# One decoding step with its gradients: ScalarE issues the stores that Pool issued, TensorE's instructions stand in written order, and a group's output sums follow a head's o sums

## The chip, the cores and the metric

The kernel runs on one core of a Trainium2 chip. A core has five engines, each with an instruction stream of its own: TensorE (PE; its weight loads appear as PEld) multiplies matrices into the PSUM accumulators, VectorE (DVE) and ScalarE (ACT) work elementwise and reduce, GpSimd (Pool) and SyncE (SP) do little but issue transfers here. Sixteen DMA engines move data between the device memory and the on-chip memory SBUF. An instruction on one engine that needs another's result waits for a semaphore, and whatever stands behind it on its own engine waits with it.

The metric is the time of one execution on the device in microseconds: 738.34 us in the median of three runs, 738.0 to 738.96.

## The reference

One token attends over a cache of 8192 positions with 32 heads, beside a gated MLP, and all gradients are wanted. With D = 640, Dh = 128, F = 1728, all bf16:

```python
xn = layernorm(x)
q  = (xn @ wq) per head                      # wq [640, 32*128]
p  = softmax(q . k_cache[h] * Dh**-0.5)      # k_cache, v_cache [32, 8192, 128]
o  = p @ v_cache[h]
out = x + concat(o) @ wo + (silu(xn @ w1) * (xn @ w3)) @ w2
# outputs: out, and the gradients of x, k_cache, v_cache, wq, wo, w1, w3, w2 for a given grad_out
```

For one head the gradients of the caches are outer products: dV[j] = p[j] * do, where do is the head's share of grad_out through wo, and dK[j] = u[j] * q, with u[j] = p[j] * (dp[j] - sum(p * dp)) and dp = V . do. K, V, dK and dV have 2 MB each per head, so per head 4 MB are read and 4 MB written. All weights are read once and a gradient of their size is written.

## The kernel before

**Layout.** A head's K lies in SBUF as 128 partitions x 64 positions x 128 elements, each partition one contiguous run of 16384 B in memory; V, dK and dV are alike. K has three buffers (`kp`) and V two (`vp`); dK and dV share four (`op`, tag "o", tile `ot`), in which W2's parts stand at the start.

**A head.** `product` (L333) forms scores: VectorE multiplies half of K (or V) by the broadcast q (or do) into `T` (L347), and TensorE adds up the 64 columns of that half with eight matmuls by the identity (L349), into `psS` or `psDP`. `row_max` and `exps` make the exponentials; ScalarE computes `E` (L392) and TensorE the total (L393). `probs` makes the probabilities `P2`, and on ScalarE `Pf` (L401). `attend` (L404) sums o with 64 matmuls over V's blocks, `row_dots` the sum p * dp (L418 on TensorE), `dscores` the vector `U2`, its copy `Uf` and 64 matmuls for dq over K's blocks (L429). `outer` (L352) writes dV or dK in two halves: of each half's 32 positions ScalarE makes eight with eight small activations (L362), VectorE the rest in one instruction (L369). `turn_wq` transposes the head's columns of Wq (L435), `weights` forms the head's rows for the weight gradients (L444 to L459), `keep_dq` stores the dq row (L465).

**The loop** (L631) runs two heads at a time, shifted: while head h is finished as `c`, the scores of head h + 1, `n`, are formed. In its order stand S of n, first half; P of c; dV first half; the sum p * dp and o; the Wq transposes; S second half; dV second half; `dscores`; dK first half; DP of n; dK second half; `exps(n)`; DP second half; `weights(c)`.

**Groups.** Four heads form a group. Wo is loaded per group (`load_wo`, two buffers), Wq for eight heads (`load_wq`, two buffers). Preparing the next group (`prep_steps`: q sums over Wq, L257, transposes of Wo, L247, do sums, L269) and finishing the last one are cut into steps, and `gap()` (L608) runs one step of the oldest at five marked places of a head. `finish_steps` (L296) starts in the first head of the next group: `on_sums` copies the group's o into `on` and `on_bf` and adds its 20 matmuls to the output (L292), then ScalarE overwrites Wo by its gradient, four activations (L301) and a store, and Wq by its gradient, five activations (L308), with a store after every second group. Three such stores of the last groups are put off (`late`) to head 29.

**Order.** `manual_schedule` (L98) keeps the written order on VectorE, SP, Pool and ScalarE. TensorE's order is made by the framework's scheduler, except at a few matmuls marked `keep_in_program_order`. Buffers are handed on by semaphores.

**Transfers.** SP issues all loads: x, W1, W2, W3, then Wq, Wo, K, V as buffers come free; a load waits on SP for its buffer, and later loads wait behind it. Pool issues all stores, each as soon as its tile is made, but for heads 30 and 31 (`TAIL`), whose dK and dV SP stores in halves (L374), the last group's Wo gradient (L706) and dx (L729). ScalarE issues only two small transfers, grad_out (L103) and out (L734). K 2 can be loaded only when W3's gradient has left its buffer (`load_k(2)` after the dW3 store, L600), V 1 after the dW1 store (L589).

Of the kernel before, what the change touches and what calls it, by code (L numbers as in the profile page):

```python
# [21 lines left out]
def kernel(  # L22
# [34 lines left out]
    NG = H // GH  # L57
    ORDERED = {mybir.EngineType.DVE, mybir.EngineType.SP, mybir.EngineType.Pool, mybir.EngineType.Activation}
    GW = 8
# [38 lines left out]
    with tc.manual_schedule(engines=ORDERED):  # L98
# [23 lines left out]
        def store(dst, src, later=False):  # L122
            if later:
                late.append((dst, src))
            else:
                nc.gpsimd.dma_start(dst, src)

# [154 lines left out]

        def on_sums(g):
            G_ = grp[g]
            wo_g = G_["wo"]
            on = small.tile([P, GH], F32, name="on")
            nc.scalar.copy(on[:], G_["on_ps"])
            on_bf = small.tile([P, GH], BF16, name="on_bf")
            nc.scalar.copy(on_bf[:], on[:])
            for r in range(GH):  # L290
                for ci in range(NC):
                    nc.tensor.matmul(accbank[:, OUT0 + ci:OUT0 + ci + 1], lhsT=wo_g[:, r, ci * P:(ci + 1) * P],  # L292
                                     rhs=on_bf[:, r:r + 1], start=False, stop=True, skip_group_check=True)
            return on

        def finish_steps(g):  # L296
            G_ = grp[g]
            wo_g = G_["wo"]
            on = on_sums(g)
            for r in range(GH):  # L300
                nc.scalar.activation(wo_g[:, r, :], g_bc_bf[:], ACTF.Copy, scale=on[:, r:r + 1])  # L301
                if r == 1:
                    yield
            store(dwo_v[g], wo_g[:], g == NG - 2)
            yield
            b, k = divmod(g, HB)
            for ci in range(NC):
                nc.scalar.activation(G_["wq"][:, ci, :], G_["dqbc"][:].rearrange("p h d -> p (h d)"),  # L308
                                     ACTF.Copy, scale=xn_col[:, ci:ci + 1])
                if ci == 2:  # L310
                    yield
            if g < NG - HB and k == HB - 1:
                store(dwq_v[:, :, b * GW * DH:(b + 1) * GW * DH], G_["wq_all"][:], g == NG - HB - 1)
# [52 lines left out]
        def outer_v(st, vec, w2, dst, h, half, j1):  # L366
# [6 lines left out]
            if h >= H - TAIL:  # L373
                nc.sync.dma_start(dst[h][:, j0:j0 + JH, :], rows[:, j0:j0 + JH, :])  # L374
            elif half:
                nc.gpsimd.dma_start(dst[h], rows)  # L376

# [92 lines left out]
        def mlp_steps():  # L470
# [13 lines left out]
            def gate_sums(wi, wt):  # L484
                for b, rows in blocks:
                    for ci in range(NC):
                        mm = nc.tensor.matmul(gu_ps[0:rows, wi, b:b + 1], lhsT=wt[:, ci, b * P:b * P + rows],
                                              rhs=xn_col_bf[:, ci:ci + 1], start=(ci == 0), stop=(ci == NC - 1))
                        if wi:
                            tc.keep_in_program_order(mm)  # L490

# [56 lines left out]

            def w2_grad(k):
                b0, nb, nfull, w2c = w2_parts[k]  # L550
                for b, rows in blocks[b0:b0 + nb]:
                    for ci in range(NC):
                        nc.tensor.matmul(accbank[:, OUT0 + ci:OUT0 + ci + 1], lhsT=w2c[0:rows, b - b0, ci * P:(ci + 1) * P],
                                         rhs=hcol_bf[0:rows, b:b + 1], start=False, stop=True, skip_group_check=True)
                    nc.scalar.activation(w2c[0:rows, b - b0, :], g_bc_bf[0:rows, :], ACTF.Copy, scale=hcol[0:rows, b:b + 1])
                    if b in (1, 3, 5, 7, 9):
                        yield
                nc.gpsimd.dma_start(dw2_v[:, b0:b0 + nfull, :], w2c[:, 0:nfull, :])
                if nfull < nb:
                    nc.gpsimd.dma_start(out_8[NF * P:F, :], w2c[0:REST, nfull, :])  # L560

# [37 lines left out]
            grad_v(1, w3t, 4, 1)  # L599
            nc.gpsimd.dma_start(dw3_v, w3t[:])  # L600
            load_k(2)
# [29 lines left out]
        for h in range(H - 1):  # L631
# [32 lines left out]
            if n:  # L664
                exps(n)
                product(n, "DP", 1)
            weights(c)
# [28 lines left out]
        keep_dq(c)  # L696
        on = on_sums(g)
        outer(c, c.q, c.U2, None, dkc, H - 1, 1)
# [66 lines left out]
```

## Time and profile before

| | before |
|---|---|
| median of three runs | 738.34 us (738.0 to 738.96) |
| profiled execution, span | 739.3 us, 0.13% above the median; the profile gives no other time of it |
| moved | 303.69 MB (151.34 MB read and as many written), 411 GB/s in the mean |
| DVE | 627.9 us busy, 85% |
| PE | 550.8 us, 75% |
| ACT | 469.0 us, 63% |
| POOL | 45.7 us, 6% |
| dK and dV stores issued by Pool | 60, 533 ns each, 19.4 us from issue to landing (median) |
| loads of K, of V on SP | 32 each, 25.4 and 21.4 us to landing |

A profile shows one execution. Its slices cut the span in 40 equal parts; a digit is the busy share of a slice in tenths. A group of instructions is named by its line, engine and tiles, output before input. A row of waits names the waiting group, an arrow and what it waited for, then the us in total, how often and the longest. The chain follows the work that ended last back through what released each step. A landing is the time from the issue of a transfer until its completion reached the semaphore.

The page's list of DMA queues has one by hardware (q1), fed by SP, one by software (q0), fed by Pool, and a second one by hardware (q10) with the two small transfers of ScalarE. The trace also has every DMA packet with queue, size and duration, and every completion count of a transfer; a transfer that uses all 16 DMA engines has 16 such counts, the last of them is its landing.

### The profile page before, as it was taken

What the parts mean: (1) busy time and instruction counts of PE and PEld (TensorE: products, weight loads), DVE (VectorE), ACT (ScalarE), POOL (GpSimd) and SP (SyncE); (2) the same over time, 40 slices, a digit from 0 to 9 for tenths busy, and PEclk for the clock granted to TensorE, in tenths of its full rate; (3) what the DMA queues carried; (4) which work ended last, traced back from release to release, by engine and by line L of the source; (5) the groups of instructions that cost most, each with busy time, mean ns of one, the idle gap of its engine ahead of it and who ended that gap; (6) DMA issues with size and microseconds to landing.
All of it is one profiled execution on the core that took longest, in us unless ns stands there. A gap on an engine that the chain in (4) does not pass through costs nothing.

```text
span 739.3 us, 15756 instructions
## 1 busy us (share of the span) xinstructions
PE 550.8 (75%) x6497; PEld 323.2 (44%) x6513; DVE 627.9 (85%) x708; ACT 469.0 (63%) x1395; POOL 45.7 (6%) x87
## 2 busy tenths in 40 slices
PE   4777787777778888685488976788188888789671
PEld 3454444434435454343255444445055444445340
DVE  3689999989699997998389996999469998899992
ACT  2394567686567774694366964686167866668552
POOL 0010000000000100000000100000000000000100
PEclk9697888777976787658696698867687678866875
DMA  9999999999999999999999999999989999999995
GB/s 325 418 396 318 402 430 429 430 425 430 428 432 427 426 430 429 427 431 424 396 402 424 426 431 426 426 433 422 429 341 418 427 425 434 426 430 425 418 413 204
DMA packets 28390, 303.69 MB, mean 411 GB/s; under 512 B 2861, under 2 KB 4591, under 8 KB 10911
## 3 DMA queue, kind: packets, MB, share of 16 engines
q1 hardware_dynamic: 16514, 160.39, 52.3%
q0 software_dynamic: 11792, 142.30, 45.7%
q8 instruction: 51, 0.84, 0.4%
q14 instruction: 21, 0.16, 0.1%
q10 hardware_dynamic: 12, 0.00, 0.0%
HBM read 151.34 MB, written 151.34 MB: 409 GB/s over the span
## 4 chain that ended last, share of the span: by engine, by line
DMA 59%; DVE 23%; PE 13%; SPq 2%; issue 1%; ACT 1%; DVEq 0%; ACTq 0%
DMA Kt<-in_A_k_cache_dram 30%; DMA out_dram<-wo_g 12%; DVE T L347 11%; DMA wq_g<-in_A_wq_dram 8%; DVE ot L369 8%; PE psS L349 5%; DMA out_dram<-ot 5%; DMA wo_g<-in_A_wo_dram 4%; PE ob L407 2%; PE ob L429 1%; DVE DP_sb L414 1%; DVE S_sb L380 1%; PE dx_ps L569 1%; SPq L152 1%; PE ps_t L247 1%
## 5 line engine op out<-in xcount | busy, mean ns | idle before, releaser
L349 PE MATMUL psDP<-T,ident_bf 128*128 128x512 bf16 x512 | 184.6, 523 | 64.8 <-DVE T L347 64.8
L349 PEld LDWEIGHTS <-ident_bf 128*128 128x128 bf16 x1024 | 121.0, 121 | 233.3 <-issue 178.8
L362 ACT ACTIVATE ot<-qs_g,Uf 128x128 bf16<-128x128 bf16 x496 | 151.5, 389 | 34.4 <-DVE Uf L427 26.4
L347 DVE TENSOR_TENSOR T<-Kt,qs_g 128x4096 bf16<-128x4096 bf16 x64 | 146.4, 2289 | 21.7 <-DMA Kt<-in_A_k_cache_dram 20.5
L349 PE MATMUL psS<-T,ident_bf 128*128 128x512 bf16 x512 | 146.5, 438 | 19.0 <-DVE T L347 18.9
L362 ACT ACTIVATE ot<-do_g,Pf 128x128 bf16<-128x128 bf16 x504 | 153.9, 389 | 1.0
L347 DVE TENSOR_TENSOR T<-Vt,do_g 128x4096 bf16<-128x4096 bf16 x64 | 145.9, 2280 | 8.8 <-DMA Vt<-in_A_v_cache_dram 8.8
L369 DVE TENSOR_TENSOR ot<-qs_g,U 128x3072 bf16<-128x3072 bf16 (+1 forms) x64 | 113.1, 1768 | 6.1 <-DMA out_dram<-ot 6.1
L369 DVE TENSOR_TENSOR ot<-do_g,P 128x3072 bf16<-128x3072 bf16 (+1 forms) x64 | 112.8, 1762 | 1.1
L376 POOL DMA_DIRECT2D out_dram<-ot x60 | 32.0, 533 | 584.3 <-DVE Uf L427 247.3
L429 PEld LDWEIGHTS <-Kt 128*128 128x128 bf16 x2048 | 58.8, 100 | 12.6 <-issue 10.9
L429 PE MATMUL ob<-U,Kt 128*128 128x1 bf16 x2048 | 58.0, 164 | 1.6 <-DVE U L422 1.5
L407 PEld LDWEIGHTS <-Vt 128*128 128x128 bf16 x2048 | 57.3, 98 | 0.0
L407 PE MATMUL ob<-P,Vt 128*128 128x1 bf16 x2048 | 57.2, 163 | 0.0
L401 ACT ACTIVATE Pf<-E,rZ 128x16 f32<-128x16 f32 x32 | 9.8, 307 | 57.4 <-DVE rZ L397 57.3
L448 ACT ACTIVATE dq_diag<-ident_bf,odq 128x128 bf16<-128x128 bf16 x32 | 12.8, 399 | 47.7 <-DVE odq L444 47.7
L392 ACT ACTIVATE E<-S_sb,negM 128x64 f32<-128x64 f32 x32 | 11.0, 345 | 41.5 <-DVE negM L389 41.5
L422 DVE SCALAR_TENSOR_TENSOR U<-DP_sb,sm,P 128x128 bf16<-128x128 f32 x32 | 11.1, 348 | 27.3 <-PE sm L418 27.3
L257 PE MATMUL ps_q<-wq_g,xn_col_bf 128*128 128x512 bf16 x32 | 11.3, 469 | 30.4 <-DMA wq_g<-in_A_wq_dram 29.4
L384 PE MATMUL sm<-ident_f,mrow 128*128 128x128 f32 x64 | 19.6, 399 | 16.9 <-DVE mrow L382 16.4
L252 ACT COPY woT<-ps_t 128x512 bf16<-128x512 bf16 x40 | 22.9, 573 | 14.2 <-PE ps_t L247 14.2
L393 PEld LDWEIGHTS sm<-rsum,ones_fc 128*128 128x128 f32 x64 | 18.2, 298 | 19.4 <-ACT E L392 12.0
(151 smaller groups left out, 508.3 us busy)
## 6 DMA issues: line engine op xcount, KB each, us to landing
out_dram<-ot POOLq DMA_DIRECT2D x60, 2048.0 KB, 19.4
Kt<-in_A_k_cache_dram SPq DMA_DIRECT2D x32, 2048.0 KB, 25.4
Vt<-in_A_v_cache_dram SPq DMA_DIRECT2D x32, 2048.0 KB, 21.4
out_dram<-ot SPq DMA_DIRECT2D x8, 1024.0 KB, 12.1
wq_g<-in_A_wq_dram SPq DMA_DIRECT2D x4, 1280.0 KB, 35.1
wo_g<-in_A_wo_dram SPq DMA_DIRECT2D x8, 640.0 KB, 10.9
out_dram<-wo_g POOLq DMA_DIRECT2D x7, 640.0 KB, 21.3
out_dram<-wq_g POOLq DMA_DIRECT2D x3, 1280.0 KB, 30.9
```

The costliest lines, as they stand in the source:

```text
L252: nc.scalar.copy(woT[:], ps_t[:])
L257: nc.tensor.matmul(ps_q[:], lhsT=xn_col_bf[:, ci:ci + 1].to_broadcast([P, P]), rhs=wq_g[:, ci, :], start=(ci == 0), stop=(ci == NC - 1))
L347: nc.vector.tensor_tensor(T[:], src[:, :, ds_], vec[:, ds_].unsqueeze(1).to_broadcast([P, J, DHH]), ALU.mult)
L349: nc.tensor.matmul(ps[:], lhsT=ident_bf[:], rhs=T[:, :, RUN * i:RUN * (i + 1)], start=(half == 0 and i == 0), stop=(half == 1 and i == DHH ...
L362: nc.scalar.activation(st.ot[:, j1 - ACT_J + j].rearrange("p a b -> p (a b)"), vec, ACTF.Copy, scale=wf[:, half, j:j + 1])
L369: nc.vector.tensor_tensor(st.ot[:, j0:j1], vec.rearrange("p (a b) -> p a b", b=2).unsqueeze(1).to_broadcast([P, n, DH // 2, 2]), w2[:, j0: ...
L376: nc.gpsimd.dma_start(dst[h], rows)
L384: nc.tensor.matmul(st.sm[:, 8:8 + P], lhsT=mrow[:].to_broadcast([P, P]), rhs=ident_f[:], start=True, stop=True, skip_group_check=True)
L393: nc.tensor.matmul(st.sm[:, 3:4], lhsT=ones_f, rhs=rsum[:], start=True, stop=True, skip_group_check=True)
L407: mm = nc.tensor.matmul(st.ob[:, 0:1], lhsT=st.V[:, j, :], rhs=st.P2[:, j, 0:1], start=(j == 0), stop=(j == J - 1), skip_group_check=True)
L429: nc.tensor.matmul(st.ob[:, 1:2], lhsT=st.K[:, j, :], rhs=st.U2[:, j, 0:1], start=(j == 0), stop=(j == J - 1), skip_group_check=True)
L448: nc.scalar.activation(dq_diag[:], ident_bf[:], ACTF.Copy, scale=odq[:, 1:2])
```

## The change

TensorE joins the engines whose order is the written one, and the marks go. Every store that Pool issued is issued by ScalarE. The stores of dV and dK are not issued where the half is made: `outer_v` notes them in `made`, and `store_made` issues them behind `dscores` and behind `exps`. Of `on_sums` the two copies become `on_cols`, at the first step of `finish_steps`, which ends there; its 20 matmuls are noted in `behind_o` and issued by `attend` behind the 64 o sums of the same head. The Wo gradient and its store so come one step later, and the five Wq activations share one step. In the MLP W2's output sums stand together ahead of W2's gradients.

```diff
-    ORDERED = {mybir.EngineType.DVE, mybir.EngineType.SP, mybir.EngineType.Pool, mybir.EngineType.Activation}
+    ORDERED = {mybir.EngineType.PE, mybir.EngineType.DVE, mybir.EngineType.SP, mybir.EngineType.Pool, mybir.EngineType.Activation}
...
         def store(dst, src, later=False):
...
-                nc.gpsimd.dma_start(dst, src)
+                nc.scalar.dma_start(dst, src)
...
-        def on_sums(g):
-            G_ = grp[g]
-            wo_g = G_["wo"]
+        behind_o = []
+
+        def on_cols(g):
             on = small.tile([P, GH], F32, name="on")
-            nc.scalar.copy(on[:], G_["on_ps"])
+            nc.scalar.copy(on[:], grp[g]["on_ps"])
             on_bf = small.tile([P, GH], BF16, name="on_bf")
             nc.scalar.copy(on_bf[:], on[:])
+            return on, on_bf
+
+        def on_sums(g, on_bf):
+            wo_g = grp[g]["wo"]
             for r in range(GH):
                 for ci in range(NC):
                     nc.tensor.matmul(accbank[:, OUT0 + ci:OUT0 + ci + 1], lhsT=wo_g[:, r, ci * P:(ci + 1) * P],
                                      rhs=on_bf[:, r:r + 1], start=False, stop=True, skip_group_check=True)
-            return on
...
         def finish_steps(g):
             G_ = grp[g]
             wo_g = G_["wo"]
-            on = on_sums(g)
+            on, on_bf = on_cols(g)
+            behind_o.append((g, on_bf))
+            yield
+            assert not behind_o
             for r in range(GH):
                 nc.scalar.activation(wo_g[:, r, :], g_bc_bf[:], ACTF.Copy, scale=on[:, r:r + 1])
                 if r == 1:
...
                                      ACTF.Copy, scale=xn_col[:, ci:ci + 1])
-                if ci == 2:
-                    yield
...
             elif half:
-                nc.gpsimd.dma_start(dst[h], rows)
+                made.append((dst[h], rows))
+
+        made = []
+
+        def store_made():
+            while made:
+                nc.scalar.dma_start(*made.pop(0))
...
-                mm = nc.tensor.matmul(st.ob[:, 0:1], lhsT=st.V[:, j, :], rhs=st.P2[:, j, 0:1], start=(j == 0),
-                                      stop=(j == J - 1), skip_group_check=True)
-                if j == 0:
-                    tc.keep_in_program_order(mm)
+                nc.tensor.matmul(st.ob[:, 0:1], lhsT=st.V[:, j, :], rhs=st.P2[:, j, 0:1], start=(j == 0),
+                                 stop=(j == J - 1), skip_group_check=True)
+            while behind_o:
+                on_sums(*behind_o.pop(0))
...
-            def w2_grad(k):
-                b0, nb, nfull, w2c = w2_parts[k]
+            for b0, nb, nfull, w2c in w2_parts:
                 for b, rows in blocks[b0:b0 + nb]:
                     for ci in range(NC):
                         nc.tensor.matmul(accbank[:, OUT0 + ci:OUT0 + ci + 1], lhsT=w2c[0:rows, b - b0, ci * P:(ci + 1) * P],
                                          rhs=hcol_bf[0:rows, b:b + 1], start=False, stop=True, skip_group_check=True)
+
+            def w2_grad(k):
+                b0, nb, nfull, w2c = w2_parts[k]
+                for b, rows in blocks[b0:b0 + nb]:
                     nc.scalar.activation(w2c[0:rows, b - b0, :], g_bc_bf[0:rows, :], ACTF.Copy, scale=hcol[0:rows, b:b + 1])
...
-                nc.gpsimd.dma_start(dw2_v[:, b0:b0 + nfull, :], w2c[:, 0:nfull, :])
+                nc.scalar.dma_start(dw2_v[:, b0:b0 + nfull, :], w2c[:, 0:nfull, :])
...
-            nc.gpsimd.dma_start(dw1_v, w1t[:])
+            nc.scalar.dma_start(dw1_v, w1t[:])
...
-            nc.gpsimd.dma_start(dw3_v, w3t[:])
+            nc.scalar.dma_start(dw3_v, w3t[:])
...
             dscores(c)
+            store_made()
             outer(c, c.q, c.U2, c.Uf, dkc, h, 0)
...
             if n:
                 exps(n)
+                store_made()
                 product(n, "DP", 1)
...
-        on = on_sums(g)
+        on, on_bf = on_cols(g)
+        on_sums(g, on_bf)
         outer(c, c.q, c.U2, None, dkc, H - 1, 1)
```

More of the change, by code (lines that the diff above doesn't have):

```diff
@@ L486, in gate_sums @@
                     for ci in range(NC):
[L487 to L490, printed above, removed]
+                        nc.tensor.matmul(gu_ps[0:rows, wi, b:b + 1], lhsT=wt[:, ci, b * P:b * P + rows],
+                                         rhs=xn_col_bf[:, ci:ci + 1], start=(ci == 0), stop=(ci == NC - 1))
             gate_sums(0, w1t)
@@ L557, in w2_grad @@
                         yield
-                nc.gpsimd.dma_start(dw2_v[:, b0:b0 + nfull, :], w2c[:, 0:nfull, :])
+                nc.scalar.dma_start(dw2_v[:, b0:b0 + nfull, :], w2c[:, 0:nfull, :])
                 if nfull < nb:
-                    nc.gpsimd.dma_start(out_8[NF * P:F, :], w2c[0:REST, nfull, :])
+                    nc.scalar.dma_start(out_8[NF * P:F, :], w2c[0:REST, nfull, :])
             dx_ps = ps_w.tile([P, NC, DR1], F32, name="dx_ps", tag="w")
```

## The prediction

> **What bounds the kernel now.** I read the forty slices of the page first, then the chain, then the waits of the engine that was to take over the work, then ten-microsecond windows where the slices dip.
>
> ```profile
> span 739.3 us, 15756 instructions
> ...
> DMA  9999999999999999999999999999989999999995
> GB/s 325 418 396 318 402 430 429 430 425 430 428 432 427 426 430 429 427 431 424 396 402 424 426 431 426 426 433 422 429 341 418 427 425 434 426 430 425 418 413 204
> ...
> q1 hardware_dynamic: 16514, 160.39, 52.3%
> q0 software_dynamic: 11792, 142.30, 45.7%
> ...
> DMA 59%; DVE 23%; PE 13%; SPq 2%; issue 1%; ACT 1%; DVEq 0%; ACTq 0%
> ```
>
> The DMA engines are at nine tenths in nearly every slice and move 425 to 434 GB/s where nothing disturbs them; the two queues together hold 98.0% of the sixteen engines' span. So 303.69 MB set the time. At 428 GB/s they need 709.5 us; the other 30 us are the dips: the first four slices, slices 20 and 30, and the last.
>
> ```profile
> ACT Pf L401 <- DVE rZ L397: 57.3, 28, 4.7
> ACT dq_diag L448 <- DVE odq L444: 47.7, 26, 3.3
> ...
> ACT E L392 <- DVE negM L389: 41.5, 25, 4.7
> ...
> PE ps_q L257 <- DMA wq_g<-in_A_wq_dram: 29.4, 3, 15.6
> DVE U L422 <- PE sm L418: 27.3, 2, 14.8
> ACT ot L362 <- DVE Uf L427: 26.4, 22, 2.2
> ...
> ACT wo_g L301 <- PE accbank L292: 5.6, 7, 0.8
> ```
>
> Each row gives us in total, times and the longest. ScalarE waits for VectorE 173 us in four of them. The rows of `ps_q` and `U` are one event seen twice: TensorE stands at a group's q sums until Wq has landed, and VectorE waits for the small sum behind it. What that costs the DMA engines is in the windows (columns from the left: stretch, busy us of PE, PEld, DVE, ACT, POOL, granted clock, DMA share, GB/s):
>
> ```profile
> 360.00:370.00 10.00, 8.47 (x94) 4.69 (x95) 2.19 (x3) 5.81 (x17) 0.53 (x1) 0.66 0.89 374
> 370.00:380.00 10.00, 7.59 (x99) 4.75 (x98) 8.38 (x9) 5.64 (x18) 0.53 (x1) 1.00 0.99 388
> ...
> 540.00:550.00 10.00, 9.18 (x169) 6.65 (x169) 6.66 (x7) 7.45 (x23) 0.53 (x1) 0.96 0.80 303
> 550.00:560.00 10.00, 7.77 (x98) 4.61 (x97) 9.79 (x13) 6.06 (x21) 0.53 (x1) 1.00 1.01 393
> ```
>
> Against 428 these four lack 54, 40, 125 and 35 GB/s for 10 us each: 2540 GB/s x us, or 5.9 us of transfer. VectorE's 111 us of idle time otherwise cost little, since transfers go on beneath them.
>
> **The change, part by part.** My sum is made against the profiled span, 739.3 us, 0.13% over the median of the runs, 738.34; I add the same terms to the median.
>
> *78 stores move from Pool to ScalarE* (60 `ot`, 7 Wo, 4 Wq, `dwq_t`, 4 of W2, W1 and W3). SP's rows of like shape give the price of an issue: 0.33 us for whole rows, 0.58 for the Wq shape. 70 x 0.33 + 8 x 0.58 = 28 us more on ScalarE, 469 becomes 497 (67%). Pool's issues (0.53 us each) leave an engine that nobody waits for. On the path I count 0: the dV store waits for VectorE's second half of dV, and ScalarE's next work waits anyway for `Uf`, which VectorE makes later; the dK store stands behind `E`, which waits for `negM`, also made later. The cover is the 173 us above. It is thin in the first head of each group, where ScalarE also makes a group's Wo and Wq gradients (10.00 busy of 10 us at 490 to 500); there the 1.3 us of the three or four issues and the two Wq activations moved to the last step make the next head's `Pf` about 2 us late, and the 2.06 us that ScalarE then waits for `Uf` takes it. SP's own issues took 1.22 us at 173, 2.2 to 2.8 at 15 to 20, and once 5.48, so an issue can hold its engine; both ends stay in the range.
>
> *The stores go from the software queue to a hardware queue.* The trace's packet records have the dWq stores as 1280 packets of 4096 B at 163.7 ns on the software queue, and the dW2 stores as 432 of 5120 B at 205.6 ns. SP's loads of the same shapes go as 2048 B at 85.8 ns and 1280 B at 60.0 ns. By those rows dWq becomes 1920 packets of 2048 B and 1280 of 1024 B (51 ns, extended from the other two): 230.5 us instead of 209.5; dW2 becomes 1728 x 60.0 = 103.7 instead of 88.8. Together 35.9 us over 16 engines, +2.2 us, on the path because the engines are the bound. Ends: 0 if ScalarE's queue packs as Pool's did, +3 if the 1024 B packet costs the 60 ns of the next larger. I take 2.2, the row of the same kind of queue. dK, dV and dWo keep 16384 and 5120 B in both queues (611 and 196 ns each), so they cost the same. The Trainium skill, "DMA: Bandwidth & Descriptors", section "Issuing engines are not separate DMA queues", says that transfers run on the same 16 engines whichever engine starts them, and that only the starting engine's time changes. Read so, this term would be 0 and the time 738.9; the packet records differ by queue, and I go by them.
>
> *Start.* ScalarE now stands at the dW1 store until VectorE has finished W1's gradient (43.4 us, some 0.8 us of waiting) and issues dW2 four times: the dW3 store, issued at 56.64, comes about 3.3 us later. SP's load of K 2 waits for its landing (69.18). V 1, issued at 55.27, keeps the engines working till 66.6 and dW3 shares them, so the sum of both ends nearly where it did. 0 to +3.3, taken as +0.3.
>
> *Tail.* Three late stores (dWq, dWo, dWq) stood behind head 29's dK on Pool, at 690.45 to 691.67; now they are issued ahead of it. dK 29's buffer is written again at 717.8 by head 31; its own landing, 707.3, moves behind 88 small packets per engine. The last of Pool's late stores had 15 of 16 engines done at 715.4 and the last one at 725.9, so VectorE may wait 0 to 8 us; but the engine that ends the kernel is working off a backlog then (below), which hides some 5 of these. +0.3, ends 0 and +3. ScalarE reaches `E` of head 30 some 2 to 3 us late; VectorE was waiting 1.28 us for K there, and `rZ` needs the sum only 5 us later: 0.
>
> *TensorE by hand.* Written order and traced order differ little: the five Wq transposes (0.44 us at full clock) go from before the S matmuls to behind the o sums, a group's turns and do sums shift by one place, the 20 out sums go from the middle of the 64 o sums to their end. W2's 70 out sums already ran together (34.2 to 36.5 us). The q sums stay where they were, so both waits for Wq stay. Behind the o sums the transposes delay the second S half by 0.3 to 0.6 us: against 0.8 us of slack in the head at 558 us, against none in the first heads of groups (at 409.2 `S_sb` starts as its last product ends). 7 x 0.6 = 4 us of VectorE's time, hidden by a head's 19.5 us of transfers (8.39 MB at 430): 0, ends -0.5 and +2.
>
> *Out sums behind the o sums.* ScalarE loses the 5.6 us of waits for them (`wo_g` row above) in seven groups. It gains nothing on the path: 0. The dWo store is issued one step later, about 6 us. SP's wait for it (L138, 126.4 us in six waits) follows the landing, not the issue, since the dV store ahead of it in the queue lands 13 us or more after its own issue. 0, ends 0 and +2.
>
> Sum: 2.2 + 0.3 + 0.3 = +2.8: 742.1 in the profiled execution's terms, 741.1 against the median. I predict 741.1 us, alone 739 to 744.
>
> **The rivals.** *A, a lagging engine was the software queue's fault* (faster). At the end 15 of 16 engines have landed everything at 732.75 us and the last at 737.34; K 31 waits 7.4 us for its last engine too. If stores by hardware queue lose that lag, the end comes 4.6 us sooner: 741.1 - 4.6 = 736.5, with 733 to 737.5 for ends met on the way. For it: dWq stores show the largest lag (30.95 us against 17.74 for the fifteenth, issued at 418.93). Against: K loads lag as well, and the lag grows after each standstill, in packets that take up to twice their 611 ns or more on either queue (90th percentile 1139 ns on the software queue at 541 to 548 us, 1412 on the hardware queue at 70 to 76). It decides once the last two counts lie within 1 us. The Trainium skill, on the page named above, section "Latency and other measured facts", holds two engines to be slower with stores by GpSimd, as a best guess through their descriptor ring, and none such by the hardware path. The trace cannot tell which engine lags.
>
> *B, Wq lands sooner* (faster). While 16384 B stores are queued, Wq's 2048 B packets take turns with them one for one: at 512 to 526 us the packet records give the software queue 372 GB/s and the loads 50. If ScalarE's stores shared otherwise, both long waits would shrink and the 5.9 us come back: 735.2, 729 to 736. Against: two hardware queues would have to share unlike hardware with software. The Trainium skill, "DMA: Bandwidth & Descriptors", section "Queues, rings and completion order", has every engine take turns between queue rows packet by packet; the shares just told agree, and by it this rival is out.
>
> *C, ScalarE held at its issues* (slower). If half of them took 2.5 us as SP's crowded ones did, the first heads of seven groups would have 3 x 2.5 us less the 2.06 of cover, some 5 us; VectorE's mean idle of 3.5 us a head (111 / 32) covers most, half of the heads paying: 7 x 1.5 / 2 = 5: 746, 744 to 752. It decides at a mean issue over 1 us. For it: the rows at 15 to 20 us. Against: SP's other issues, at 0.33 to 0.66 beside equal backlogs.
>
> *D, the tail is not covered* (slower): dK 29 late by 8 us, 5 us of it at the end: 746.
>
> *E, nothing moves*: packed as before, start and tail hidden: 738.3, within 1.5 us.
>
> **How the numbers follow.** Forecast 0.42, A 0.14, B 0.09, C 0.14, D 0.07, E 0.14. 0.2% is 1.5 us, about what a measurement here can tell from no change (the three runs lie within 0.96 us). Of the forecast's own range 0.05 falls within it, and of A nothing of weight: slower 0.37 + 0.14 + 0.07 = 0.58, same 0.05 + 0.14 = 0.19, faster 0.14 + 0.09 = 0.23. The range 733 to 748 leaves out most of B's lower half and C's upper half and the tails, under 0.2.
>
> **What would show it.** Packets should rise from 28390 by some 3200, all in dWq and dW2, with the software queue gone and its 142.30 MB on another hardware queue. ScalarE's issues should lie at 0.33 to 0.6 us, `Pf` in the heads 4, 8 and so on later, with no new VectorE wait. Slices 20 and 30 should dip as before. The forecast is wrong if slice 30 recovers (B), if the last engine lands with the others (A), if issue rows of ScalarE exceed 1 us (C), or if VectorE waits for `ot` near 717 (D).

## The result, and the profile after

The changed kernel takes 742.18 us (median of 20 runs, 739.99 to 743.62) where the kernel before took 740.21 beside it (20 runs, 737.63 to 741.68): a ratio of 1.0030 with a 95% interval of 1.0019 to 1.0041. A second series gave 741.70 against 739.60, 1.0031 (1.0019 to 1.0043). It is slower by 0.3%: the medians differ by 2.0 and 2.1 us, the ratio means 2.2. 741.1 was predicted, 2.8 above the 738.34 of before. The cause is not the term that carried the prediction.

First the page of the changed kernel, with the lines that answer to those of before.

```profile
span 738.6 us, 15713 instructions
...
DMA  9999999999999999999999999999999999999995
GB/s 330 419 404 350 398 426 431 429 427 430 429 429 431 420 430 428 432 425 425 389 395 427 427 427 428 429 427 426 426 363 427 428 427 429 431 427 430 419 379 194
DMA packets 31606, 303.69 MB, mean 411 GB/s; under 512 B 2861, under 2 KB 7599, under 8 KB 14127
## 3 DMA queue, kind: packets, MB, share of 16 engines
q1 hardware_dynamic: 16514, 160.39, 52.2%
q10 hardware_dynamic: 15020, 142.30, 45.8%
...
DMA 5%; DVE 1%; PE 0%; issue 0%; DVEq 0%
```

Three things are to be seen. The software queue is gone, and its 142.30 MB are on q10, ScalarE's, in 3216 packets more than before. Slices 20 and 30 dip as they did, and the last two are lower (379 and 194; 413 and 204 before). And the chain, which had gone back through the whole kernel, is 6% of the span long: it begins at a single transfer of 36 us. The span is *shorter* than the 739.3 of before, though the kernel is slower. In every run that lists both, the time is 1.7 to 2.2 us above the span (here 740.72 against 738.6), so the execution profiled before took some 741.4 us, more than the median of its kernel, and this one took less than the median of its own. A second profile of each has 737.2 (before) and 738.6 (after). One profile of each kernel can't show a difference of 2 us in the spans; it can show waits that one kernel has and the other has not.

The waits of the changed kernel, in the columns of the prediction's rows:

```profile
ACT Pf L411 <- DVE rZ L407: 42.3, 20, 5.1
ACT E L402 <- DVE negM L399: 36.1, 26, 4.3
...
PE ps_q L257 <- DMA wq_g<-in_A_wq_dram: 30.0, 3, 14.8
...
DVE U L432 <- PE sm L428: 25.4, 2, 12.7
ACT ot L366 <- DVE Uf L437: 25.2, 29, 2.2
DVE ot L373 <- DMA out_dram<-ot: 24.7, 3, 8.4
```

and the row of before that answers to the last one:

```profile
DVE ot L369 <- DMA out_dram<-ot: 6.1, 3, 3.0
```

TensorE's waits for Wq and VectorE's behind them are what they were (29.4 and 27.3). What has grown is the last row: VectorE waits three times, 24.7 us in all, for stores to land so that it may write `ot` again (6.1 us in three waits before). Two of the three lie at 290 and 463 us, where the engines move 425 GB/s or more all the same. The third is the one at the head of the chain (first the chain, then ScalarE's issues, then VectorE's timeline, and last VectorE's timeline before):

```profile
687.65 36.26 DMA out_dram<-ot
```

```profile
682.62 0.57 ACTq L126 DMA_DIRECT2D out_dram<-wq_g  x1
...
683.21 0.79 ACTq L126 DMA_DIRECT2D out_dram<-wo_g  x1
...
684.04 0.54 ACTq L126 DMA_DIRECT2D out_dram<-wq_g  x1
...
687.65 3.22 ACTq L386 DMA_DIRECT2D out_dram<-ot  x1
```

```profile
715.33 0.35 DVE L432 SCALAR_TENSOR_TENSOR U<-DP_sb,sm,P 128x128 bf16<-128x128 f32 x1
724.00 2.29 DVE L373 TENSOR_TENSOR ot<-qs_g,U 128x4096 bf16<-128x4096 bf16 x1 [8.31 <-DMA out_dram<-ot]
```

```profile
717.76 2.29 DVE L369 TENSOR_TENSOR ot<-qs_g,U 128x4096 bf16<-128x4096 bf16 x1
```

ScalarE issues head 29's dK at 687.65, behind the three late stores, and it lands 36.26 us later; before, it was issued at 689.93 and landed at 707.33. It is one DMA engine of the sixteen that makes it late (the trace doesn't tell which): fifteen of the sixteen completion counts of this dK are there at 707.92, the last at 723.91. On the 88 small packets ahead of it the same is seen: of the third late store fifteen counts are there at 700.60, the last at 716.31. VectorE stands 8.31 us for the buffer, and SP's last stores go out that much later. What the transfers do meanwhile, in ten-microsecond windows (share of the DMA engines and GB/s in the last two columns), first after, then before:

```profile
710.00:720.00 10.00, 6.11 (x151) 4.89 (x150) 5.51 (x9) 4.11 (x13) 0.00 (x0) 0.77 0.86 353
720.00:730.00 10.00, 1.36 (x28) 1.00 (x27) 5.97 (x9) 3.25 (x9) 0.00 (x0) 0.50 0.33 134
730.00:740.00 10.00, 0.82 (x3) 0.51 (x3) 1.47 (x11) 1.03 (x2) 0.00 (x0) 0.50 0.60 223
```

```profile
710.00:720.00 10.00, 7.62 (x156) 5.81 (x155) 9.75 (x13) 4.21 (x15) 0.00 (x0) 0.84 0.99 406
720.00:730.00 10.00, 2.17 (x31) 1.51 (x30) 5.45 (x19) 4.29 (x10) 0.84 (x1) 0.50 0.99 389
730.00:740.00 10.00, 0.00 (x0) 0.00 (x0) 0.00 (x0) 0.00 (x0) 0.00 (x0) 0.50 0.06 21
```

After, the engines run dry at 720 to 730 us and make up for it at 730 to 740. The stretch from VectorE's first product of K 31 to the end compares profiles without what came before it: 46.0 and 45.5 us in the two profiles of before (693.32 to 739.3, 691.75 to 737.2), 47.3 and 47.1 after (691.27 and 691.47 to 738.6).

### The profile page after: what moved, and what is told of

The parts are those of the page before. It is cut to its first block, busy times and chain, and to the rows that moved or that the text cites. A ratio compares the mean times of both kernels' runs of the same rounds, so it can differ in the third digit from the quotient of the medians.

```text
span 738.6 us, 15713 instructions
## 1 busy us (share of the span) xinstructions
PE 546.7 (74%) x6513; PEld 323.1 (44%) x6513; DVE 626.9 (85%) x708; ACT 469.6 (64%) x1395; POOL 1.7 (0%) x9
## 3 DMA queue, kind: packets, MB, share of 16 engines
q10 hardware_dynamic: 15020, 142.30, 45.8%
## 5 line engine op out<-in xcount | busy, mean ns | idle before, releaser
L353 PE MATMUL psDP<-T,ident_bf 128*128 128x512 bf16 x512 | 175.3, 504 | 61.2 <-DVE T L351 61.1
L353 PE MATMUL psS<-T,ident_bf 128*128 128x512 bf16 x512 | 149.7, 445 | 12.5 <-DVE T L351 12.5
L458 ACT ACTIVATE dq_diag<-ident_bf,odq 128x128 bf16<-128x128 bf16 x32 | 12.9, 402 | 65.9 <-DVE odq L454 63.0
L428 PE MATMUL sm<-rdot,ones_fc 128*128 128x1 f32 x64 | 12.3, 262 | 38.2 <-DVE junk L427 38.2
L257 PE MATMUL ps_q<-wq_g,xn_col_bf 128*128 128x512 bf16 x40 | 12.5, 453 | 30.0 <-DMA wq_g<-in_A_wq_dram 30.0
L428 PEld LDWEIGHTS sm<-rdot,ones_fc 128*128 128x128 f32 x64 | 10.2, 200 | 49.6 <-DVE junk L427 49.6
L390 DVE TENSOR_REDUCE S_sb<-psS 128x64 f32<-128x512 f32 x32 | 21.9, 685 | 8.7 <-PE psS L353 8.6
```

The lines of the kernel that those rows point to most:

```text
L257: nc.tensor.matmul(ps_q[:], lhsT=xn_col_bf[:, ci:ci + 1].to_broadcast([P, P]), rhs=wq_g[:, ci, :], start=(ci == 0), stop=(ci == NC - 1))
L353: nc.tensor.matmul(ps[:], lhsT=ident_bf[:], rhs=T[:, :, RUN * i:RUN * (i + 1)], start=(half == 0 and i == 0), stop=(half == 1 and i == DHH ...
L390: nc.vector.tensor_reduce(st.S[:], st.ps["S"][:], AX.X, ALU.add)
L428: nc.tensor.matmul(st.sm[:, 4:5], lhsT=ones_f, rhs=rdot[:], start=True, stop=True, skip_group_check=True)
L458: nc.scalar.activation(dq_diag[:], ident_bf[:], ACTF.Copy, scale=odq[:, 1:2])
```

## The experiments

Theory 1: the place of the late stores ahead of dK 29 makes the loss. Theory 2: the smaller packets make it. Theory 3: TensorE's written order makes it. All ratios below are to the kernel before, run beside it.

**What the comparison can tell.** Two runs were for that: the changed kernel again (1.0031, given above), and the kernel before against itself.

> The changed kernel itself once more, beside the others of this series: a ratio of 1.002 to 1.004 to the kernel before, and a second profile of it. The first profile's execution (740.72 us) lay below all but one of its timed runs, so this one should be 1 to 2 us longer; theory 1 (tail) expects the wait of about 8 us for dK 29's landing again, and under 300 GB/s at 720 to 730 us.

> The kernel before, word for word, against itself: a ratio of 0.999 to 1.001, which is what the comparisons here can tell from no change, and a second profile of it. If the changed kernel's earlier start is real (the engines lack 12.2 us of transfer by 90 us in the profile before, 10.3 and 10.0 in the two of the changed kernel), this one shows 11.5 to 13 again; if it is chance, 10 to 11.

Before against itself: 738.12 against 739.68, a ratio of 0.9983 (0.9968 to 0.9998). The interval leaves out 1, so differences up to some 0.2% must not be read as effects, whatever their interval says. The 0.3% of the change, measured twice, is above that, but not by much. The second profile of the changed kernel has the same wait, 8.03 us. The start was chance: by 90 us the engines lacked 10.3 us of transfer against 428 GB/s in the second profile of before too, as in both of the changed kernel (10.3, 10.0), not 12.2.

**The order in the tail.** Three edits bear on it. The late stores behind dK 29 (run twice):

```diff
-            if h == H - 3:
-                for dst, src in late:
-                    store(dst, src)
...
                 exps(n)
                 store_made()
+            if h == H - 3:
+                for dst, src in late:
+                    store(dst, src)
+            if n:
                 product(n, "DP", 1)
```

> The changed kernel with one thing moved: the three late stores (two of dWq, one of dWo) are issued behind head 29's dK store instead of ahead of it. Theory 1 (the tail makes the loss: VectorE waits 8.3 us at 715.7 to 724.0 for dK 29's landing and the engines then run dry at 720 to 730 us): the wait at dK 31 falls below 1 us, dK 29 lands near 707 us, the store of the last pieces is issued near 721 instead of 728.8, and the time falls by 3 to 5 us against the changed kernel, to a ratio of 0.993 to 0.998 against the kernel before. Theory 2 (the smaller packets of dWq and dW2 make it): the wait goes too, but the time stays at a ratio of 1.002 to 1.004, since these packets and their 0.7 us are the same. Theory 3 (the written order of TensorE makes it): 1.003 as well.

> The changed kernel with the late stores behind dK 29 once more, beside the run above: a ratio of 1.000 to 1.002 (1.0014 before), no wait of VectorE for dK 29, and from VectorE's first product of K 31 to the end 45.5 to 47 us, as in the kernel before (46.0 and 45.5), against 47.3 and 47.1 in the changed kernel.

Measured: 740.43 us, 1.0014 (1.0001 to 1.0028), and in the second series 740.07, 1.0007 (0.9997 to 1.0016). The wait is gone, as in this line of the second run, where the same product starts as soon as VectorE is free:

```profile
715.61 0.35 DVE L432 SCALAR_TENSOR_TENSOR U<-DP_sb,sm,P 128x128 bf16<-128x128 f32 x1
715.99 2.29 DVE L373 TENSOR_TENSOR ot<-qs_g,U 128x4096 bf16<-128x4096 bf16 x1
```

Theory 1 had put 3 to 5 us on it, and that is a miss: from 1.0030 to about 1.001 is 1.5 us. From K 31's product to the end it took 46.9 and 46.3 us. TensorE's written order and the small packets are in these two runs as well, so together with all else that is left of the change they cost some 0.1% here.

A likely reason for the miss is in the waits of SP's queue (SPq) in the first run:

```profile
SPq L378 <- DMA out_dram<-wq_g: 8.0, 1, 8.0
```

SP's third-last store of `ot` has its data at 716.92 and goes out at 722.86, 0.08 us after a late dWq store has landed (fifteen of its engines at 706.14, the last at 722.78). It doesn't need that store; the two are on the same completion semaphore, as SP and ScalarE share eight in the changed kernel. The store behind it goes out 0.06 us after the landing of dWo, on a second shared one, and the last pieces at 724.65 (722.84 in the second run, where SP stands 7.1 us) instead of near 721. At 710 to 720 and 720 to 730 us the engines move 316 and 273 GB/s, where before they moved 406 and 389. So one wait for a lagging engine went and another came; what the edit would give back without the second one wasn't tried.

The late stores where the change has them, but issued by Pool:

```diff
             if h == H - 3:
                 for dst, src in late:
-                    store(dst, src)
+                    nc.gpsimd.dma_start(dst, src)
```

> The changed kernel with one thing changed: the three late stores, at their place ahead of head 29's dK, are issued by Pool, which has no other store, so that dK 29 no longer stands behind them in a queue, though all of them move at the same time. Theory 1a (dK 29 lands late because it stands behind them in its queue, on the lagging engine above all): it lands before 715 us, VectorE's wait falls below 1 us, and the ratio is 1.000 to 1.002, as with the late stores moved behind it. Rival 1b (it lands late because the engines are busy with them, whichever queue): it lands after 718 us, VectorE waits 3 us or more, and the ratio stays at 1.0025 to 1.004.

Measured: 740.39 us, 1.0004 (0.9993 to 1.0015). Pool, which has nothing else to do, issued them at 593.68, 673.14 and 678.81, each as soon as its data were there, and they had landed at 617.93, 689.42 and 702.89. dK 29 was issued at 692.95, landed at 714.30 and came in time (VectorE's timeline):

```profile
723.36 0.35 DVE L432 SCALAR_TENSOR_TENSOR U<-DP_sb,sm,P 128x128 bf16<-128x128 f32 x1
723.74 2.29 DVE L373 TENSOR_TENSOR ot<-qs_g,U 128x4096 bf16<-128x4096 bf16 x1
```

So dK 29 is in time where it doesn't stand behind the late stores, whether they come later in its queue (it lands 18.5 and 17.5 us after its issue there) or go by another. That it is the queue's order alone, and not that the engines are busy with the small packets, this run doesn't show: only the last of the three was still moving beside dK 29. The Trainium skill, "DMA: Bandwidth & Descriptors", section "Queues, rings and completion order", says that a DMA engine takes a queue's descriptors in their order and goes round the queues by packets. For the first half, 36.26 us behind the late stores and 18.5 ahead of them agree. Something is paid elsewhere in this run: VectorE waits for K 31 and starts on it at 699.14 instead of 691 to 693, and the rest then takes 41.0 us instead of 47. That this is because the late stores took the engines earlier is likely, as the bytes are the same, but it wasn't tried.

And the same order in the kernel before, where nothing else of the change is made:

```diff
+            elif half and h == H - 3 and dst is dkc:
+                made.append((dst[h], rows))
             elif half:
                 nc.gpsimd.dma_start(dst[h], rows)
...
                 for dst, src in late:
                     store(dst, src)
+                nc.gpsimd.dma_start(*made.pop())
```

> The kernel before with one thing changed: head 29's dK store is issued by Pool behind the three late stores instead of ahead of them. Theory 1 (the tail's order costs what moving it back gave in the changed kernel, 1.0030 to 1.0014): VectorE waits 4 to 9 us for dK 29's landing, and the ratio is 1.001 to 1.003. Rival: the wait comes, but the engines still work off their backlog then and the ratio is 0.999 to 1.001.

Measured: 742.20 us, 1.0041 (1.0023 to 1.0059). Pool's timeline and VectorE's:

```profile
682.84 0.87 POOL L126 DMA_DIRECT2D out_dram<-wq_g  x1
683.52 0.73 POOL L126 DMA_DIRECT2D out_dram<-wo_g  x1
684.06 1.06 POOL L126 DMA_DIRECT2D out_dram<-wq_g  x1
689.18 0.55 POOL L667 DMA_DIRECT2D out_dram<-ot  x1 [4.06 <-issue]
```

```profile
723.93 2.29 DVE L369 TENSOR_TENSOR ot<-qs_g,U 128x4096 bf16<-128x4096 bf16 x1 [7.04 <-DMA out_dram<-ot]
```

With the packets of before and the engines' order of before, this order alone costs 3.0 us (1.7 to 4.4). Here too it is one engine: fifteen counts of dK 29 are there at 708.99, the last at 723.84. From K 31's product to the end it takes 49.8 us (692.47 to 742.3) instead of 46.0 and 45.5, but the execution profiled was the slowest of the eight, 2 us above their median, so this stretch may be too long. Taken away, the order gives back 1.6 us (1.00305, the mean of two, less 1.0008, the mean of the three runs without the wait), put in it costs 3.0: theory 1 holds, with a size of 1.6 to 3 us. (1.6 us by itself is at the edge of what these comparisons tell; the wait in the traces and the 3.0 us carry it.) What is left of the change, 1.0004 to 1.0014, can't be told from nothing.

**The packets.** The late dWo store behind dK 29, and dWq, `dwq_t` and dW2 issued by Pool again, so that their packets have 4096 and 5120 B as before. (The edit moves the late dWq stores too, but Pool issues them as soon as their data are there, at 595.38 and 680.71, as in the run above.)

```diff
+            elif dst.shape[-1] >= GH * DH and len(dst.shape) == 3 and dst.shape[1] == NC:
+                nc.gpsimd.dma_start(dst, src)
             else:
                 nc.scalar.dma_start(dst, src)
...
-                nc.scalar.dma_start(dw2_v[:, b0:b0 + nfull, :], w2c[:, 0:nfull, :])
+                nc.gpsimd.dma_start(dw2_v[:, b0:b0 + nfull, :], w2c[:, 0:nfull, :])
```

> The late stores behind dK 29 as in the run above, and in addition the four dWq stores, dwq_t and the four of dW2 issued by Pool, so that their packets are 4096 and 5120 B again; dK, dV and dWo stay with ScalarE. Theory 2 (packets): 2 us or more below the kernel with the late stores moved alone. Theory 1: within 1 us of it, since the packets' summed time differs by 0.7 us an engine only (dWq 13.1 against 13.9, dW2 and dWo 17.1 against 17.0). Packets: 28390.

Measured: 742.31 us, 1.0038 (1.0023 to 1.0054), with 28389 packets. That is against both: with the large packets the kernel is 1.9 us slower than without, not faster. TensorE waits 12.5 us for Wo here (2.9 with ScalarE's stores), the engines lack 12.9 us of transfer by 90 us (12.0 there), and VectorE starts on K 31 only at 699.20; which of it makes the 1.9 us isn't settled. As more than the packets changed, this run by itself doesn't refute theory 2. What speaks against it are the two runs above, with the small packets in place and 1.0014 and 1.0007, and the packet records: the dWq stores take 10.15 + 3.79 us an engine in the changed kernel and 13.1 before, dW2 with dWo 16.97 and 17.07, together +0.7 us (+1.4 between the second profiles of the two kernels).

**The two halves of the change alone.** TensorE in written order and the out sums behind the o sums, every store by Pool at its old place (dW1, dW2 and dW3 like the two shown):

```diff
             elif half:
-                made.append((dst[h], rows))
+                nc.gpsimd.dma_start(dst[h], rows)
...
             else:
-                nc.scalar.dma_start(dst, src)
+                nc.gpsimd.dma_start(dst, src)
```

> One part alone: TensorE in its written order with the out sums behind the o sums, but all stores issued by Pool at their old places. Theory 1 (tail) and theory 2 (packets): a ratio of 0.999 to 1.001, 28390 packets, no wait of VectorE for dK 31's buffer over 1 us. Theory 3 (TensorE's order makes the loss): 1.003.

Measured: 742.92 us, 1.0049 (1.0034 to 1.0064). By the number theory 3 seems to win, but the trace shows another cause. First Pool's, then SP's, then TensorE's timeline:

```profile
414.91 0.53 POOL L380 DMA_DIRECT2D out_dram<-ot  x1 [6.33 <-ACT wo_g L307]
415.45 0.53 POOL L126 DMA_DIRECT2D out_dram<-wo_g  x1
```

```profile
437.41 0.33 SPq L138 DMA_DIRECT2D wo_g<-in_A_wo_dram  x1
```

```profile
448.22 0.61 PE L247 MATMUL ps_t<-ident_bf,wo_g 128*128 128x128 bf16 x4 [9.16 <-DMA wo_g<-in_A_wo_dram]
```

With the out sums a step later, Pool issues dWo behind the head's dK, 2 MB, instead of ahead of it (409.80 before, and 412.31 in the changed kernel, where dK follows at 412.75). Wo, which waits for dWo's landing, is loaded at 437.41 instead of 429.71 (427.42 in the changed kernel), and TensorE stands at Wo's transposes: 35.1 us in four waits, 4.2 before. That points to dWo's place in its queue, which the next run moves:

```diff
             while made:
-                nc.scalar.dma_start(*made.pop(0))
+                nc.gpsimd.dma_start(*made.pop(0))
```

and likewise at every other store of the changed kernel.

> The changed kernel with every store issued by Pool at the very place in the program where ScalarE issues it, so that dWo stands ahead of the head's dK in the queue (with TensorE in written order and the stores at Pool's old places, dWo stood behind dK, Wo was loaded 5 to 8 us later, TensorE stood 8 to 9 us at Wo's transposes and the ratio was 1.0049). Theory 4 (the place of dWo's store in its queue makes that loss, not the engine that issues it): Wo's loads are issued within 3 us of the changed kernel's, TensorE waits under 4 us for Wo, and the ratio falls to 0.999 to 1.003. Theory 5 (Pool's queue itself is slow to land small stores beside large ones): TensorE still waits 5 us or more for Wo and the ratio stays at 1.004 to 1.005.

Measured: 744.54 us, 1.0066 (1.0053 to 1.0079). TensorE's wait came as theory 4 has it, 1.4 us or less for Wo; Wo's load goes out at 431.77, 4.4 us after the changed kernel's (the other five 1.5 to 3.0 us after).

```profile
417.27 0.53 POOL L126 DMA_DIRECT2D out_dram<-wo_g  x1 [6.53 <-ACT wo_g L307]
417.80 0.53 POOL L386 DMA_DIRECT2D out_dram<-ot  x1
```

```profile
441.75 0.40 PE L247 MATMUL ps_t<-ident_bf,wo_g 128*128 128x128 bf16 x4 [0.30 <-DMA wo_g<-in_A_wo_dram]
```

The ratio did not: my expectation had forgotten that this kernel has the late stores ahead of dK 29 as well (VectorE waits 5.42 us for it), which by itself made 1.0041. The other 0.25% is open; the engines lack 4.7 us of transfer at 340 to 400 us here and 2.6 before, but 3.4 and 3.9 in the two profiles of the changed kernel. So the wait for Wo is shown to come from dWo's place, but how much of the 0.5% it makes is not: without it the time did not fall. At the same places, stores by ScalarE are 0.35% faster than by Pool (1.0031 against 1.0066, in one series). The Trainium skill, on the page named above, section "Issuing engines are not separate DMA queues", has the choice of the engine save only the time of issuing. No engine waits for Pool's time of issuing, so by that rule the two should be about equal, and here they are not. The packets and the moments of issue differ too; which of it makes the difference is open.

The other half: the stores by ScalarE, TensorE's order by the scheduler, the out sums where they were.

```diff
-    ORDERED = {mybir.EngineType.PE, mybir.EngineType.DVE, mybir.EngineType.SP, mybir.EngineType.Pool, mybir.EngineType.Activation}
+    ORDERED = {mybir.EngineType.DVE, mybir.EngineType.SP, mybir.EngineType.Pool, mybir.EngineType.Activation}
```

with `on_sums`, `attend` and the marks for the order as before.

> The other part alone: the stores issued by ScalarE, TensorE's order left to the scheduler and the out sums where they were. Theories 1 and 2: a ratio of 1.002 to 1.005 with 31606 packets and the wait of 8 us for dK 29's landing. Theory 3: 0.999 to 1.001.

Measured: 840.96 us, 1.1358 (1.1332 to 1.1385), which no theory had. The waits:

```profile
ACT dqbc_g L471 <- PE ps_db L456: 114.4, 24, 5.3
...
DVE rZ L403 <- PE sm L399: 104.1, 32, 7.8
...
ACT woT L252 <- PE ps_t L247: 84.0, 16, 9.8
```

Once the stores are among ScalarE's instructions, the scheduler orders TensorE otherwise: the eight psS products of the next head stand ahead of the sum that `rZ` needs (302.69 and 304.41 in one head), and `ps_db`, which ScalarE reads, behind the second half of psS. VectorE waits in every head for `rZ` (there is no such row before), and ScalarE, in its order, with `ot` columns behind `dqbc_g`: 3 us a head. So the two halves can't be added: one alone costs 0.5%, the other 13.6%, both together 0.3%.

**The waits for Wq.** The prediction put 5.9 us of lost transfer on them. Two kernels take them away, both with the late stores behind dK 29: Wq loaded two heads earlier by SP, and the same by Pool.

```diff
-                if (g + 1) % HB == 0 and g + 1 > HB:
-                    load_wq((g + 1) // HB)
...
+            if hh == 2 and g % HB == 0 and 0 < g < NG - HB:
+                load_wq(g // HB + 1)
```

> The changed kernel with the late stores behind dK 29 (ratio 1.0014 by itself) and Wq of the next eight heads loaded two heads earlier. If the transfers lost around TensorE's two long waits for Wq (5.9 us by the windows at 360 to 380 and 540 to 560 us) are lost for good: both waits fall below 3 us, those windows come to 415 GB/s or more, and the time falls by 4 to 6 us, to a ratio of 0.993 to 0.997. Rival: the waits go, but the gap comes back elsewhere (start or tail), 1.000 to 1.002.

> The changed kernel with the late stores behind dK 29 (1.0014 by itself), and the last two Wq loads issued by Pool, which issues nothing else there, as soon as their buffer is free, so that no load and no store stands behind them in a queue. With SP issuing them two heads earlier TensorE no longer waited, but VectorE stood 7.6 and 7.4 us for the V loads behind them, the engines ran dry one to three heads later (362 and 369 GB/s at 380 to 400 us, 318 at 560 to 570), and the ratio was 1.0046. If what costs is the queue standing behind Wq's 2048 B packets, these dips go as well as the waits: 412 GB/s or more from 340 to 600 us, and a ratio of 0.993 to 0.998. Rival: three queues taking turns slow the others by as much, and the ratio stays at 1.001 to 1.005.

Measured: 742.73 us, 1.0046 (1.0029 to 1.0063), and 742.97, 1.0047 (1.0028 to 1.0065). TensorE waits for Wq no more, and both kernels are slower. With SP's loads, VectorE's line is

```profile
326.78 2.29 DVE L351 TENSOR_TENSOR T<-Vt,do_g 128x4096 bf16<-128x4096 bf16 x1 [7.61 <-DMA Vt<-in_A_v_cache_dram]
```

and the dip comes 20 us later (columns as above):

```profile
360.00:380.00 20.00, 15.52 (x200) 9.55 (x199) 14.32 (x14) 11.44 (x35) 0.00 (x0) 0.83 1.01 419
380.00:400.00 20.00, 15.37 (x181) 8.76 (x181) 19.71 (x22) 12.83 (x40) 0.00 (x0) 0.83 0.95 366
```

In the run with SP's loads ScalarE, too, is held: two of its dK stores go out at 285.51 and 460.06, 0.1 us after the landing of the dWq store before them on the same shared semaphore, and its work behind them stands 8.33 and 6.08 us.

```profile
285.91 0.40 ACT L458 ACTIVATE dq_diag<-ident_bf,odq 128x128 bf16<-128x128 bf16 x1 [8.33 <-DMA out_dram<-wq_g]
```

With Pool's, V is in time, but Wo is late by 6.3 and 6.1 us, and the dips are at 380 to 400 (396 GB/s) and 540 to 580 (388, 387). In the first run the waits go and the ratio is above that of theory and rival; in the second the ratio is the rival's, though what the rival gives as its reason wasn't tried by itself. Wq's 2048 B packets are not what the two share: by Pool the two loads went as 640 packets of 4096 B. That another load pays where TensorE did fits both; why is open.

No kernel tried here beats the kernel before; the best two, in which dK 29 doesn't stand behind the late stores, equal it.

## Why the prediction was right, and where it was not

The time and its sign were right: +2.8 us were summed up, +2.0 to +2.2 measured. Two terms of the sum were wrong, one too large and one too small, and they nearly cancel. That the sum came so near is luck.

- **Base.** The sum was set against 739.3 us as if the span were the time, "0.13% over the median". The time is 2 us longer, so that execution was 0.4% over it. The median of three runs, 738.34, was itself low: the same kernel had 739.20 to 740.26 beside the others later (738.12 once, when it ran against itself). The difference of 2.8 us holds without the base; as an absolute time, 741.1 is 1 to 2 us low for it.
- **Packets, +2.2.** The count came as worked out, 3216 more, the size didn't: +0.7 us an engine, or +1.4 by the second profiles. ScalarE's 1280 B packets took 55.2 ns where SP's loads took 60.0, the 1024 B ones 47.4 instead of 51, the 2048 B ones 84.6 instead of 85.8. And the 205.6 ns that the prediction gave dW2's packets on the software queue are the mean of them and dWo's; dW2's alone took 222.6 (dWo's 197.4), so more was saved there than it counted. In the time 0.7 us is 0.1%, which the two runs with the packets in place (1.0014, 1.0007) can't tell from nothing.
- **Tail, +0.3 with ends of 0 and +3.** This is the step that failed. The mechanism was there, the landing "moves behind 88 small packets per engine" and "VectorE may wait 0 to 8 us", and so was the number: 8.31 us. But the text took 5 of them for hidden and then nearly all the rest as well. Measured are 1.6 to 3 us, so 5 to 7 of the 8 were hidden, and what was left over was nearer to the end of the range than to 0.3. It is hidden at the end: from the start of VectorE's last product to the end it takes 12.1 us instead of 19.1 and 18.5, as less backlog is in the way of the last stores; 3.9 us of it are the last engine's, which ends 4.6 us behind the fifteenth before and 0.7 us behind it now.
- **Rival D.** Its event, dK 29 late by 8 us, came, and the forecast had named a VectorE wait near 717 as a sign that it is wrong: by its own list the tail was refuted, and the time was not. Its time of 746 added 5 us to the forecast's other terms; the event was worth 1.6 to 3, and the packets weren't there.
- **ScalarE, 0, and rival C.** Right. The 60 stores took 338 ns in the median, and all 80 issues 424 in the mean. Two took over 1 us: a dW2 store, 1.13, and dK 29 itself, 3.22, behind the late stores with their small packets.
- **Start, +0.3.** The dW3 store was issued 2.5 us later (59.17 for 56.64), as said, but landed earlier (67.11 for 69.18). The second profile of before shows that starts vary by as much anyway: no cost to be seen.
- **TensorE by hand, 0; out sums, 0.** Right for the change as a whole, not borne out for the TensorE half alone (0.5%). That the dWo store, a step later, costs nothing was argued from its landing behind dV; here ScalarE issues it ahead of dK and TensorE waits 3.2 us for Wo, and where it stands behind dK TensorE waits 35.1 us and the kernel takes 0.5% more; how much of that is the wait is open.
- **Rival A** (the lag belongs to the software queue) is out: of ScalarE's late dWq store, issued at 682.62, fifteen engines had landed at 697.4 and the last at 706.4, and the same lag makes dK 29 late. At the very end, the sign that it named did come: the last two counts lie 0.7 us apart (4.6 before). But they do so as well in the kernel before with dK 29 behind the late stores, where Pool's queue has both, so it isn't the queue that makes it; there and here the engines ran dry shortly before. **Rival B** is out by the waits for Wq, and its 5.9 us weren't to be had by other means tried here. **Rival E** had the packets packed as before; they weren't.

## What to carry to other kernels

Where stores share a queue, their order in it is a schedule: a store that another engine waits for must not stand behind small ones, and a move of all stores to another engine is to be read for such inversions, one by one. A wait near the end is worth what is left after the backlog that it lets drain; price it by the stretch from the last common event to the end, not by its own length. Where queues share completion semaphores, a store can also be held by the landing of one that it has nothing to do with; that is read from the issuing engine's own waits. And a difference of 0.3% needs the same kernel against itself and a pair of edits, one that takes the suspect away and one that puts it into the other kernel.

## What was not expected

- The kernel before against itself gave 0.9983 with an interval of 0.9968 to 0.9998.
- SP's V loads came to wait for transfers that they have nothing to do with, the loads and stores of Wq. These rows of SP's queue are new after the change, where the trace has SP's and ScalarE's transfers on the same eight semaphores; Pool's had eight of their own before. In the changed kernel itself no cost of it is seen. In two of the runs above such a wait holds back SP's last stores (8.0 us) or ScalarE (8.33 and 6.08 us). A kernel with the semaphores kept apart wasn't tried.

```profile
SPq L115 <- DMA wq_g<-in_A_wq_dram: 30.2, 2, 15.3
...
SPq L115 <- DMA out_dram<-wq_g: 25.6, 2, 13.0
```

- Small packets hold up what stands behind them in their queue, in mid-kernel too: the waits for `ot` at 290 and 463 us follow the dWq stores issued at 244.00 and 417.99, the second 8.43 us long. The longest of their kind in the two profiles of before are 4.1 us, and the kernel of the run on the packets, with dWq issued by Pool, has none. There they cost nothing that is seen; at the end of the kernel the like of it cost 1.6 to 3 us.
